# New latencies in the planner of an attention and MLP kernel, and its static rules chosen anew

## The chip, the cores and the metric

The kernel runs on one core of a Trainium2 chip. The time is that of the device for one execution, in microseconds (us), the median of several runs. Lower is better.

## The reference

The input is a sequence x of 2048 rows of 640 values in bf16. What is computed is x + s * g.

```
xn = layernorm(x)
q, k, v = split(xn @ wqkv)                 # 32 heads of 20 values
s  = softmax(q k^T / sqrt(20)) v @ wo      # attention, per head 2048 x 2048 scores
u  = gelu(layernorm(xn)^T @ w1 + b1)       # MLP over the rows (2048 -> 1536 -> 2048)
g  = silu((u @ w2 + b2)^T)
out = x + s * g
```

## The kernel before

**The work.** The 32 heads form 8 groups of 4 heads; a *pass* is one group and 512 query rows, and there are 33 passes, the last two of half a pass each. A pass goes through 16 chunks of 128 keys. One head, one chunk and 512 queries make a *unit*: a score product of 128 x 512 that fills one PSUM bank. There are 2,048 units. The four heads of a group lie in the four row strips of TensorE (PE), so that up to four units with different heads run side by side.

**Two ways through a unit.** Most units (1,552) go to ScalarE (ACT): one activation takes the exponential of two or three banks (`emit_exp`, L1308) into `pt_sb`, a ring of 20 tiles. The other 496 go to VectorE (DVE): `emit_op1` (L1319) makes 16-bit integers out of one bank that are read as bf16 values of an approximate exponential, and `emit_top` (L1357) makes three shifted copies of four such units (a quad); four products with scaled values (`vs_sb`) take their weighted sum. PE then multiplies `pt_sb` and `dt_sb` by the values (`pv_mm`, L1376), with four column tiles side by side, into one accumulator bank. After a pass DVE transposes and normalizes it (`ep_steps`, L1492 to L1518).

**The banks.** Of 8 PSUM banks six form two groups of three, (0, 1, 2) and (3, 4, 5). A *visit* (`do_st`, `emit_st`, L1279) is a run of score products into one group: three units for ACT, or two for ACT and one whose bank is lent to DVE, at times with one more in bank 7. While ACT works on one group, PE may fill the other. Bank 6 is the accumulator; bank 7 serves the other products.

**The other work on PE.** Between visits PE does the value products, the projections of Q, K and V (L633, L746 before the exponentials are in full flow; L648, L691 later), both MLP layers (L648), and the output projection (L965, L970). The later projections and the MLP use column tiles too. Where PE has nothing to do, `emit_fill` (L1393) adds four products with zero weights, so that its activity does not fall; `emit_warm` (L1403) does the same ahead of the first products. `row_piece` (L656) cuts one step of a projection into four row strips and hangs one of them beside a visit.

**The order of the work.** A planner in the kernel's own Python code decides it. It keeps a clock for each engine (`Prog.T`), adds a cost for every instruction, and notes for each one when others may use what it wrote (`fin`, plus `lat` by engines). In a loop it takes the engine whose next possible instruction comes first, and that engine's candidate with the best priority. The order of each engine's instructions is fixed by this; on the chip semaphores alone hold them back. For PE, `act_deadline` gives the time by which the next visit has to begin for ACT not to run dry, and `pe_cands` offers other work only where it ends, by the planner's costs, before that.

Three terms of these costs matter here. `lat` (L66) is added between an end on one engine and a start on another. `pe_cost` (L460) adds a price where the tiling of PE changes: row strips for a visit ("st"), column tiles ("pv"), whole array ("full"). `emit_st` (L1262) spreads the time of a visit over its products, and `_add` sets the `fin` of a PE instruction to its end and 170 ns. Before the change, the first products of a visit cost 20 ns each and the last one the rest of 216 ns:

```
cost = (first if i == 0 else 0.0) + (20.0 if i < n - 1 else tot - 20.0 * (n - 1))
```

The class constants are the static rules: `D_GUARD` (units that have to be left for ACT in a pass before a new DVE quad may be started in it, and the mark for giving up bank 7 at the end), `MLP_A`, `MLP_B` (passes over which the MLP is spread), `ROOM` (free tiles in the ring below which value products come first), `FGAP` (ns of slack from which a fill is allowed), `ACTP` (priority of the MLP's activation steps), `PARTS` (pieces in which a quad's four value products may be issued), `V1A`, `V1B` (passes over which the later V projection is spread).

Of the kernel before, what the change touches and what calls it, by code (L numbers as in the profile page):

```python
# [39 lines left out]
class Prog:  # L40
# [23 lines left out]
        self.alog = []  # L64

    def lat(self, eng, src):  # L66
        return (40.0 if eng == "dve" else 0.0) if src == eng else self.LAT[eng] + (79.0 if eng == "act" and src == "pe" else 57.0 if eng == "dve" and src == "pe" else 0.0)

    def ready(self, eng, reads=(), writes=()):
        r = 0.0  # L70
# [195 lines left out]
class _Kern:  # L266
# [13 lines left out]
    AK = (1.0, 0.83984375, 0.70703125, 0.59375)  # L280
    MEAN4 = 4.159829600672171
    LOG2E = 1.4426950408889634
    D_GUARD = 8
    MLP_A, MLP_B = 2.6, 23.0
    QK_LEAD = 6.0
    SLACK, MINJ = 0.0, 640.0
    ROOM = 3
    ROWM, ROWP, ROWN = 5, 2, 400
    lastrow = None
    MERGE = False  # L290
# [10 lines left out]
    LONE, DLEAD, DRIDE = False, 0.0, 400.0  # L301
    NQS = 3
    CONFL = True
    FILL, FGAP, FACT = True, 40.0, 0.6
    LATE = 1.0
    LEND, LEND_MIN = 1800.0, 3
    SHARE = True
    VPRIO = 25.0
    QAT = (0.0, 0.0, 0.0, 0.0)
    ACTP = 22.0  # L310
    COLS = True
    NTILE, NLIVE, EARLY = 8, 3, True
    QC = ((0.5, 3.0), (3.2, 6.4), (9.0, 13.5), (14.0, 18.0), (19.0, 22.0))
# [6 lines left out]
        ("MINJ", (640.0, 320.0, 1000.0)),  # L320
        ("ROOM", (3, 6, 0)),
        ("DRIDE", (400.0, 150.0, 700.0)),
        ("LEND", (1800.0, 1300.0, 2400.0, 700.0, 0.0)),
        ("PARTS", ((2,), (2, 1), (3, 1), (1,), ())),
        ("LATE", (2.0, -9.0, 99.0)),
# [6 lines left out]
        ("GROT", (1, 0)),  # L332
    )
    PLAN = ()
    PARTS = (2,)
    DX = (1, 2, 3)
    V1A, V1B = 1.2, 3.0

    def __init__(self, nc, A_x, A_wqkv, A_wo, B_w1, B_b1, B_w2, B_b2, out):
        self.nc = nc  # L340
# [70 lines left out]
    def schedule(self):  # L411
        pr, t, nc = self.prog, self.t, self.nc
# [28 lines left out]
        def ps(b, n=512, off=0):  # L441
            return ps_all[:, b * 512 + off:b * 512 + off + n]
# [17 lines left out]
        def pe_cost(mode, c):  # L460
            if pe_mode[0] != mode:
                pe_mode[0] = mode
                return c + max(0.0, (105.0 if mode == "st" else 113.0) - max(0.0, pr.T["pe"] - pr.pe_end))
            return c

        def dma(fn, reads, writes, name, nbytes, over=()):
# [399 lines left out]
        UP = NB * GH  # L866
# [3 lines left out]
        units, dunits = [], []  # L870
# [149 lines left out]
        bankq = []  # L1020
# [38 lines left out]
        nclaim = [0]  # L1059
# [71 lines left out]
        dop1 = []  # L1131
# [68 lines left out]
        def d_claimable():  # L1200
            if not self.DON:
                return None
            if tfree and dlive[0] < self.NLIVE:
# [3 lines left out]
                for q in (q0, q0 + 1):  # L1207
                    if q >= NP:
                        continue
                    G, p = passes[q]  # L1210
                    if q == q0 and a_left(q) < self.D_GUARD:
                        continue
# [49 lines left out]
        def emit_st(lst, banks):  # L1262
            n = len(lst)
            first = pe_cost("st", 0.0)
            gs = {}
            for (q, c, g) in lst:
                gs[g] = gs.get(g, 0) + 1
            tot = 216.0 * max(gs.values())
            for i, (q, c, g) in enumerate(lst):
                G, p = passes[q]  # L1270
                slot = G % 2
                bk = banks[i]
                cost = (first if i == 0 else 0.0) + (20.0 if i < n - 1 else tot - 20.0 * (n - 1))
                np_ = len(units[q][c])
                for ch, col, m, off, _ in units[q][c]:
                    lhsT = qk_sb[32 * g:32 * g + 32, slot, 1, ch * 128:(ch + 1) * 128]
                    rhs = qk_sb[32 * g:32 * g + 32, slot, 0, col:col + m]
                    outp = ps(bk, m, off)
                    pr.pe(lambda e, outp=outp, lhsT=lhsT, rhs=rhs, g=g: e.matmul(outp, lhsT, rhs, start=True, stop=True,  # L1279
                                                                                tile_position=(32 * g, 0)),  # L1280
                          reads=qslots(slot, p, col, m, g) + [S_(kslot(slot, ch, g))] + ([S_(f"qkp_{g}")] if slot else []),
                          writes=[bank_slot[bk]], name=f"st{q}_{c}_{g}", cost=cost / np_, w=53.0 / np_)
                nclaim[0] += 1
                if st_left[G] == NTB * UP:
                    done.add(f"STbegin{G}")
                st_left[G] -= 1
                if st_left[G] == 0:
                    done.add(f"ST{G}")
# [259 lines left out]
        for w in (1, 0):  # L1548
            src = A_wqkv[:, 640 * w + 256:640 * w + 640].rearrange("(kc p) f -> p kc f", p=P)
# [64 lines left out]
        for j in range(FC):  # L1614
# [4 lines left out]
            if j % 2:  # L1619
                add_job(f"a1_{j}", act_steps(1, j), tuple(f"m1_{i}_{q}" for i in (j - 1, j) for q in (0, 1)), self.ACTP)  # L1620
            if j % 2 == 1 and j // 2 + 2 < FC // 2:
# [5 lines left out]
        for j in range(NB):  # L1627
# [4 lines left out]
            if j % 2:  # L1632
                add_job(f"a2_{j}", act_steps(2, j), tuple(f"m2_{i}_{q}" for i in (j - 1, j) for q in (0, 1)), self.ACTP)
            if j % 2 == 1 and j // 2 + 2 < NB // 2:
                k = j // 2 + 2
                add_job(f"w2_{k}", [dma_w2(k), ("tag", f"w2_{k}")], (f"m2_{j}_0", f"m2_{j}_1"), 40.0)
        tot = sum(x[3] for x in ml)
# [10 lines left out]
        for gb in range(4):  # L1648
            src = A_x[0, gb * 512:(gb + 1) * 512, :].rearrange("(b p) d -> p b d", p=P)
# [122 lines left out]
        def pe_cands(T):  # L1772
# [110 lines left out]
            room = sum(not b for b in pt_busy) - pend  # L1883
            if room < self.ROOM:
                o = [x for x in pv if x[1] <= T + 1.0 and x[4] > 0]
# [204 lines left out]
            return a - done_cost["act"], pe - done_cost["pe"], d - done_cost["dve"]  # L2090

        self.loads = loads
        guard = 0
        win = 0
        while True:
# [10 lines left out]
            if nomore:  # L2106
                for b in act_banks:
                    if b not in bank_off and b not in lent and not any(b in x[1] for x in pexp):
                        bank_off.add(b)
                        if len(tbank) < NL:  # L2110
                            done.add(f"tbank{len(tbank)}")
                            tbank.append(b)
            if (nomore or (a_cur[0] == NP - 1 and a_left(NP - 1) < self.D_GUARD)) and d_cur[0] is None and not dop1:
                if not bankq and JB not in busybanks and JB not in bank_off:
# [18 lines left out]
            r, e = bt  # L2133
# [46 lines left out]
```

## Time and profile before

| what | us |
|---|---|
| median of 3 runs | 756.44 (756.05 to 757.03) |
| the profiled execution | 757.3 |
| its span, first to last instruction | 755.5 |
| ACT busy | 730.5, of it exponentials 711.7 (683) |
| DVE busy | 720.5 |
| PE busy | 709.7 |
| GpSimd (POOL) busy | 15.5 |

The span is the time from the first to the last instruction of the profiled execution; 1.8 us lie around it. A busy time is the union of an engine's instruction records. PE's matmuls are pipelined and their ends are modelled, so that its busy time is not a measure of how full it is. Records of successive activations overlap (the mean record of a 128x1024 exponential is 1106 ns long), so that an idle time of less than that overlap does not show in busy time, and starts have to be compared. The granted TensorE clock is 1.000 in the mean of the span.

### The profile page before, as it was taken

To read this page: it belongs to the slowest core of one execution; us is meant where nothing else is said; L and a number is where in the kernel's file an instruction comes from. 1 tells how busy PE (TensorE), PEld (TensorE's weight loads), DVE (VectorE), ACT (ScalarE), POOL (GpSimd) and SP (SyncE) were. 2 spreads that over 40 slices of the span, in tenths; PEclk is the share of its full clock that TensorE was granted. 3 is DMA by queue.
4 is the path that set the end of the run, shared out by engine and by line. 5 is a ranking of instruction groups with operands and counts; after the bars stand their busy time and mean duration, and the time that the engine had idled before them with its cause. 6 is when DMAs were issued, how large, how long until landed. Compare 5 with 4: busy or idle time off the path is not lost.

```text
span 755.5 us, 23583 instructions
## 1 busy us (share of the span) xinstructions
PE 709.7 (94%) x10508; PEld 242.5 (32%) x10520; DVE 720.5 (95%) x1321; ACT 730.5 (97%) x708; POOL 15.5 (2%) x23
## 2 busy tenths in 40 slices
PE   8889999999999999999999998999999999999997
PEld 7332222232233323332232232323233332332333
DVE  8899989999998999999999999999999999999997
ACT  5899999999999999999999999999999999999994
POOL 4200000000000000000000000000000000000000
PEclk9999999999999999999999999999999999999999
DMA  9745211110121301312011104122225510041012
GB/s 234 146 113 63 63 22 37 20 37 5 40 60 20 76 6 45 85 34 46 13 31 27 30 7 119 19 51 50 60 80 88 130 39 30 2 152 47 26 35 71
DMA packets 119738, 42.66 MB, mean 56 GB/s; under 512 B 79172, under 2 KB 118468, under 8 KB 119588
## 3 DMA queue, kind: packets, MB, share of 16 engines
q1 hardware_dynamic: 119636, 41.15, 23.6%
q8 instruction: 82, 1.34, 0.8%
q14 instruction: 20, 0.16, 0.1%
HBM read 26.37 MB, written 10.22 MB: 48 GB/s over the span
## 4 chain that ended last, share of the span: by engine, by line
ACT 84%; PE 11%; DVE 3%; DMA 1%; SPq 0%; issue 0%
ACT pt_sb L1308 82%; PE ps_all L648 4%; PE ps_all L1279 4%; PE ps_all L1376 3%; ACT zt_sb L849 1%; ACT zt_sb L844 1%; DMA regA<-in_A_x_dram 1%; DVE regC L568 1%; DMA xnT_sb<-regC 0%; PE ps_all L965 0%; PE ps_all L633 0%; DVE bst_sb L530 0%; DVE bst_sb L532 0%; DVE dt_sb L1319 0%; DVE v_sb L1114 0%
## 5 line engine op out<-in xcount | busy, mean ns | idle before, releaser
L1308 ACT ACTIVATE pt_sb<-ps_all 128x1024 bf16<-128x1024 f32 (+2 forms) x683 | 711.7, 1220 | 6.1 <-PE ps_all L1279 3.8
L1319 DVE TENSOR_SCALAR dt_sb<-ps_all 128x512 uint16<-128x512 f32 x496 | 327.7, 679 | 18.8 <-PE ps_all L1279 9.7
L1279 PE MATMUL ps_all<-qk_sb 32*128 32x512 bf16 (+1 forms) x2128 | 268.6, 376 | 32.5 <-ACT pt_sb L1308 28.9
L1357 DVE TENSOR_SCALAR dt_sb<-dt_sb 128x2048 uint16<-128x2048 uint16 x372 | 239.2, 683 | 1.6
L1279 PEld LDWEIGHTS ps_all<-qk_sb 32*128 32x128 bf16 x2128 | 68.3, 91 | 289.5 <-ACT pt_sb L1308 243.8
L1376 PE MATMUL ps_all<-pt_sb,v_sb 128*21 128x512 bf16 (+1 forms) x1616 | 127.0, 374 | 2.3 <-DVE v_sb L1114 1.0
L1376 PE MATMUL ps_all<-dt_sb,vs_sb 128*21 128x512 bf16 (+1 forms) x1536 | 124.1, 375 | 0.1
L648 PE MATMUL ps_all<-regB,regA 128*32 128x128 bf16 (+1 forms) x1492 | 63.6, 299 | 0.0
L648 PE MATMUL ps_all<-regC,regA 128*32 128x128 bf16 (+1 forms) x1448 | 62.5, 296 | 0.1
L1376 PE MATMUL ps_all<-dt_sb,v_sb 128*21 128x512 bf16 (+1 forms) x512 | 49.0, 378 | 0.3 <-issue 0.3
L1376 PEld LDWEIGHTS ps_all<-pt_sb,v_sb 128*21 128x21 bf16 x1616 | 32.9, 91 | 50.9 <-issue 32.5
L648 PE MATMUL ps_all<-xnT_sb,wqk_sb 128*32 128x512 bf16 x640 | 45.6, 382 | 0.2 <-DVE qs_sb L1117 0.2
L1376 PEld LDWEIGHTS ps_all<-dt_sb,vs_sb 128*21 128x21 bf16 x1536 | 30.0, 91 | 33.1 <-issue 22.9
L648 PEld LDWEIGHTS ps_all<-regB,regA 128*32 128x32 bf16 x1492 | 26.9, 96 | 25.2 <-issue 12.9
L648 PEld LDWEIGHTS ps_all<-regC,regA 128*32 128x32 bf16 x1448 | 26.2, 96 | 24.9 <-issue 14.0
L656 PE MATMUL ps_all<-regC,regA 32*128 32x512 bf16 x88 | 33.9, 385 | 0.0
L965 PE MATMUL ps_all<-wv_sb,xnT_sb 128*128 128x128 bf16 (+1 forms) x150 | 25.4, 296 | 1.9 <-issue 1.1
L1500 DVE STREAM_TRANSPOSE tr_sb<-ps_all 128x512 f32<-128x512 f32 x31 | 21.9, 706 | 0.0
L648 PE MATMUL ps_all<-wv_sb,xnT_sb 128*32 128x480 bf16 x320 | 21.1, 369 | 0.0
L1376 PEld LDWEIGHTS ps_all<-dt_sb,v_sb 128*21 128x21 bf16 x512 | 12.5, 90 | 24.3 <-issue 21.0
L648 PEld LDWEIGHTS ps_all<-xnT_sb,wqk_sb 128*32 128x32 bf16 x640 | 13.2, 95 | 18.4 <-issue 8.1
L823 DVE TENSOR_SCALAR zt_sb<-ps_all,b2h_sb 128x512 bf16<-128x512 f32 (+1 forms) x32 | 17.2, 540 | 0.6 <-PE ps_all L648 0.6
(88 smaller groups left out, 347.5 us busy)
## 6 DMA issues: line engine op xcount, KB each, us to landing
regA<-in_B_w_dram SPq DMA_DIRECT2D x6, 1024.0 KB
regA<-in_B_w_dram SPq DMA_DIRECT2D x8, 768.0 KB
qk_sb<-qk_scratch_dram SPq DMA_DIRECT2D x56, 80.0 KB
qk_scratch_dram<-qs_sb SPq DMA_DIRECT2D x32, 128.0 KB
regA<-in_A_x_dram SPq DMA_DIRECT2D x6, 640.0 KB
ok_scratch_dram<-on_sb SPq DMA_DIRECT2D x96, 20.0 KB
out_dram<-regC SPq DMA_DIRECT2D x3, 640.0 KB
wqk_sb<-in_A_wqkv_dram SPq DMA_DIRECT2D x2, 480.0 KB
```

What stands on the lines that cost most here:

```text
L568: steps.append(("dve", lambda e, b=b: e.tensor_scalar(regC[:, b, :], regC[:, b, :], st_sb[:, 6, b:b + 1], None, ALU.mult), [S_("r2"), S_(f ...
L648: fns.append(lambda e, c=c, e_=e_: e.matmul(oc(c, e_), lhsT[:, c:e_], rhs, start=start, stop=stop, tile_position=(0, c)))
L656: row = lambda g: (lambda e: e.matmul(oc(0, 128), lhsT[32 * g:32 * g + 32, :], rhs[32 * g:32 * g + 32, :], start=False, stop=False, tile_p ...
L823: steps.append(("dve", lambda e, z=z, i=i, jj=jj: e.tensor_scalar(z[:, c0:c0 + n], ps(bk, n, i * n), 0.5, bias[:, jj:jj + 1], ALU.mult, AL ...
L844: steps.append(("act", lambda e: e.activation(tt_, tt_, AF.Tanh, scale=1.5957691216), [stt], [stt], f"th{j}", ac(n)))
L965: steps.append(("pe", lambda e, c=c: e.matmul(ap, oT_sb[:, c, b * 128:(b + 1) * 128], wo_ap[:, c, c0:c0 + n], start=(opens and c == 0), st ...
L1279: pr.pe(lambda e, outp=outp, lhsT=lhsT, rhs=rhs, g=g: e.matmul(outp, lhsT, rhs, start=True, stop=True, tile_position=(32 * g, 0)), reads=q ...
L1308: tk = pr.act(lambda e: e.activation(outp, inp, AF.Exp, scale=math.log(2.0) / 128.0), reads=[bank_slot[b] for b in banks[:n]], writes=[S_( ...
L1319: tk = pr.dve(lambda e: e.tensor_scalar(w, src, WOFF, 0.0, ALU.add, ALU.max), reads=[bank_slot[bk]], writes=[S_(f"dt{d['tl'][0]}_{g}")], n ...
L1357: tk = pr.dve(lambda e: e.tensor_scalar(dst, src, dk, None, ALU.add), reads=[S_(f"dt{b}_{g}") for b in inb for g in range(4)], writes=[S_( ...
L1376: pr.pe(lambda e: e.matmul(outp, lhsT, rhs, start=(k == 0), stop=last, tile_position=(0, 32 * g)), reads=reads, writes=[bank_slot[AB]], na ...
L1500: steps.append(("dve", lambda e: e.transpose(tr_sb[:, :], ps(AB)), [bank_slot[AB]], [S_("tr")], f"epT{q}", 632.0))
```

## The change

It has four parts.

1. `lat`: from a PE result to ACT 95 ns instead of 134, to DVE 100 instead of 112.
2. `pe_cost`: a tiling change costs 105 ns less half of the time that PE has waited just before; it was 105 or 113 less all of that time.
3. `emit_st`: the products of a visit start 4 ns apart, and each one is taken as done 332 ns after its own start (358 where its bank is DVE's), with 216 ns more for each earlier product of the same head in the visit and with the price of the tiling change for the first one.
4. The static rules get other values. A lambda, `self.backlog`, is added that nothing in the kernel calls; the lists `OPTS` and `PLAN` have no effect, as `PLAN` is empty.

```diff
-        return (40.0 if eng == "dve" else 0.0) if src == eng else self.LAT[eng] + (79.0 if eng == "act" and src == "pe" else 57.0 if eng == "dve" and src == "pe" else 0.0)
+        return (40.0 if eng == "dve" else 0.0) if src == eng else self.LAT[eng] + (40.0 if eng == "act" and src == "pe" else 45.0 if eng == "dve" and src == "pe" else 0.0)
...
-    D_GUARD = 8
-    MLP_A, MLP_B = 2.6, 23.0
+    D_GUARD = 16
+    MLP_A, MLP_B = 2.6, 24.0
...
-    ROOM = 3
+    ROOM = 6
...
-    FILL, FGAP, FACT = True, 40.0, 0.6
+    FILL, FGAP, FACT = True, 0.0, 0.6
...
-    ACTP = 22.0
+    ACTP = 30.0
...
-    PARTS = (2,)
+    PARTS = (3, 1)
...
-    V1A, V1B = 1.2, 3.0
+    V1A, V1B = 0.5, 4.0
...
-                return c + max(0.0, (105.0 if mode == "st" else 113.0) - max(0.0, pr.T["pe"] - pr.pe_end))
+                return c + max(0.0, 105.0 - 0.5 * max(0.0, pr.T["pe"] - pr.pe_end))
...
             tot = 216.0 * max(gs.values())
+            own = {x[2] for x in dop1}
+            gs = {}
             for i, (q, c, g) in enumerate(lst):
+                late = (358.0 if banks[i] in own else 332.0) + 216.0 * gs.get(g, 0)
+                gs[g] = gs.get(g, 0) + 1
...
-                cost = (first if i == 0 else 0.0) + (20.0 if i < n - 1 else tot - 20.0 * (n - 1))
+                cost = (first if i == 0 else 0.0) + (4.0 if i < n - 1 else tot - 4.0 * (n - 1))
...
-                for ch, col, m, off, _ in units[q][c]:
+                for n_, (ch, col, m, off, _) in enumerate(units[q][c]):
...
-                    pr.pe(lambda e, outp=outp, lhsT=lhsT, rhs=rhs, g=g: e.matmul(outp, lhsT, rhs, start=True, stop=True,
+                    t = pr.pe(lambda e, outp=outp, lhsT=lhsT, rhs=rhs, g=g: e.matmul(outp, lhsT, rhs, start=True, stop=True,
...
+                    t.fin = t.t0 + late + (first if i + n_ == 0 else 0.0)
```

No line of the change issues an instruction by itself. The order of the instructions on PE, DVE, ACT and the DMA queue is another one throughout.

More of the change, by code (lines that the diff above doesn't have):

```diff
@@ L1278, in emit_st @@
                     outp = ps(bk, m, off)
-                    pr.pe(lambda e, outp=outp, lhsT=lhsT, rhs=rhs, g=g: e.matmul(outp, lhsT, rhs, start=True, stop=True,
-                                                                                tile_position=(32 * g, 0)),
+                    t = pr.pe(lambda e, outp=outp, lhsT=lhsT, rhs=rhs, g=g: e.matmul(outp, lhsT, rhs, start=True, stop=True,
+                                                                                    tile_position=(32 * g, 0)),
                           reads=qslots(slot, p, col, m, g) + [S_(kslot(slot, ch, g))] + ([S_(f"qkp_{g}")] if slot else []),
                           writes=[bank_slot[bk]], name=f"st{q}_{c}_{g}", cost=cost / np_, w=53.0 / np_)
+                    t.fin = t.t0 + late + (first if i + n_ == 0 else 0.0)
                 nclaim[0] += 1
@@ L2092, in schedule @@
         self.loads = loads
+        self.backlog = lambda: sum(1 for j in bankq if j.at <= nclaim[0] / UP)
         guard = 0
```

## The prediction

> **What bounds the kernel now.** The first view is the page: the busy line, then the chain that ended last.
>
> ```profile
> PE 709.7 (94%) x10508; PEld 242.5 (32%) x10520; DVE 720.5 (95%) x1321; ACT 730.5 (97%) x708; POOL 15.5 (2%) x23
> ACT 84%; PE 11%; DVE 3%; DMA 1%; SPq 0%; issue 0%
> ```
>
> Three engines are over 94% busy, but the chain runs along ACT for 84% of the span, nearly all of it the exponentials (L1308). Busy time hides short stalls, since an exponential's record overlaps the next one's, so the second view is the starts of successive activations in the trace. Undisturbed, a 128x1024 exponential (two score units, a "double") is followed after 903 ns and a 128x1536 one (a "triple") after 1330 ns, though their records last 1106 and 1524 ns. ACT's work is thus 495 x 0.903 + 187 x 1.330 + one single of 0.48 + 14 tanh of 1.16 = 712.4 us. The first exponential starts at 11.9 us and the last is over at 744.8: 732.9 us. With 1.1 us of copies inside, 19 us are stalls: 4.5 us before 50 us, some 14 us spread evenly after it (0.7 to 2.2 us in every 50), the rest is rounding. So there are three places to win or lose: the start, the 14 us, and the 10.7 us after the last exponential.
>
> The third view shows what such a stall is, the timeline around 61 us.
>
> ```profile
> 60.68 0.39 PE L1279 MATMUL ps_all<-qk_sb 32*128 32x512 bf16 x3
> 61.00 0.40 PE L1376 MATMUL ps_all<-dt_sb,v_sb 128*21 128x512 bf16 x4
> 61.22 0.39 PE L1376 MATMUL ps_all<-dt_sb,vs_sb 128*21 128x512 bf16 x4
> 61.44 0.60 PE L1376 MATMUL ps_all<-pt_sb,v_sb 128*21 128x512 bf16 x8
> 61.98 0.39 PE L1279 MATMUL ps_all<-qk_sb 32*128 32x512 bf16 x3
> 62.45 1.33 DVE L1319 TENSOR_SCALAR dt_sb<-ps_all 128x512 uint16<-128x512 f32 x2
> ```
>
> L1279 is a visit: three score products side by side. Four matmuls with column tiles (L1376) take 0.22 us together (61.00, 61.22, 61.44): a **slot**. From the visit to the slots after it 0.32 us pass, 0.10 more than a slot, and as much on the way back: the tiling change. The visit at 61.98 comes after four slots; ACT's next exponential starts at 62.41 in the trace, 0.43 us after it, and DVE's first step at 62.45, 0.47 after it. ACT had been free since 62.20: it stalled 0.21 us. The chain around 136 us shows the same with five slots of a projection:
>
> ```profile
> 133.18 2.27 ACT pt_sb L1308 x2
> 135.45 0.05 issue
> 135.50 0.39 PE ps_all L1279 x3
> 135.89 1.12 PE ps_all L648 x20
> 137.02 0.37 PE ps_all L1279 x3
> 137.39 3.27 ACT pt_sb L1308 x3
> ```
>
> **What the Trainium skill says.** "TensorEngine Tiling (Array Packing)", Key Properties: changing the tiling mode drains TensorE; the trace agrees, 0.10 us each way. "TensorE: Matmul & The Clock Gate", Part 3 (The mechanism): tiles on different rows start about 4 ns apart and matmuls end in program order; the trace agrees on the starts (a visit's products lie 430, 427 and 424 ns ahead of a double), and ACT's 0.43 us holds whether it reads two or three of them, so they do end together. "ScalarE: Activation LUTs", What ACT_TABLE_LOAD costs: 186 ns + 0.833 per column less 93 of overlap, an estimate of 946 ns for a double; the trace has 903 and decides.
>
> **The rule for a stall.** A bank group is free when its exponential's record ends, 1106 - 903 = 203 ns after the next one starts; the visit follows 54 ns later at the earliest, and what reads it starts 430 ns after. Between two visits PE may therefore spend the two exponentials before less 687 ns. For two doubles: 1806 - 687 - 216 (visit) - 2 x 97 (changes) = 709 ns, three slots (649). Four slots (865) are some 156 ns too many. With a triple among the two, five fit.
>
> **The change part by part.**
>
> *The planner's reckoning* (lat, pe_cost, emit_st). It issues nothing; it alters when the planner thinks banks are full. Before, the products of a visit end one after the other: for a double whose third product goes to DVE the plan has ACT ready at 20 + 20 + 170 + 134 = 344 ns, for a triple at 520. The trace has 430 and 440. The new formula gives 332 + 4 + 95 = 431 and 435; for DVE 358 + 8 + 100 = 466 against 464 to 466. So doubles, 495 of the 683 exponentials, were taken for 86 ns quicker than they are, and the plan put four slots where they do not fit. That the change of tiling hides half of a wait I can't read from a view.
>
> *The order that results*, counted in the two built orders. Work is the same: 2,128 score and 3,664 value matmuls, 496 DVE units, 14 tanh. What differs:
> - Exponentials: 491 doubles and 190 triples, no single: 443.4 + 252.7 = 696.1 against 696.2 us. One 128x512 copy (L1116) goes from DVE to ACT: +0.5. Net **+0.4**.
> - Between 30 exponentials after the start and 12 before the end, four or more slots stand between two doubles 38 times before and 21 after. I priced every interval by its kind (the two exponentials, the slots) with the mean stall that its kind has in the trace of before: four slots between doubles 32 times, 4.9 us, 153 ns each, now 17 times, 2.6 us; five or more 6 times, 0.9, now 4, 0.6; four after triple and double 19 times, 1.1, now 10, 0.6; all others 7.1, now 6.4. Sum 14.0 to 10.2: **-3.8**.
> - The remaining four-slot pieces are placed by a clock that fits: of the 32, eight cost 21 ns or less. Bounds 0 and -2.6 (none of them stalls); I take **-0.8**.
> - Tiling changes 1,257 to 1,292: 35 x 0.1 = 3.5 us more of PE. Fills (L1393) 200 to 244 matmuls, 11 slots, 2.4 us; row pieces (L656) 132 to 120, three whole steps back in the open, 0.6 us. In that middle part PE's work goes from 610 to 616 us, its reserve against ACT from 55 to 46. Cover: that reserve. If stalls grow as the reserve shrinks, 14 x (55/46 - 1) = 2.7; bounds 0 and +2.7, I take **+1.0**.
> - DVE: same steps less one; it has 712 busy of 743 us and is fed by the same visits. Nothing, as long as the visits come no later.
> - SP: the same 306 DMAs. Granted clock is full throughout before (PEclk all 9), and fills grow: nothing.
>
> *The start.* At 30.23 ACT waited 1.35 us:
>
> ```profile
> 28.02 0.49 DVE L1114 CAST v_sb<-ps_all 128x320 bf16<-128x320 f32 x1 [0.20 <-PE ps_all L746]
> 28.57 0.72 PE L633 MATMUL ps_all<-xnT_sb,wp_sb 128*128 128x256 bf16 x5 [0.59 <-DVE v_sb L1114]
> 30.23 1.45 ACT L1308 ACTIVATE pt_sb<-ps_all 128x1536 bf16<-128x1536 f32 x1 [1.35 <-PE ps_all L1279]
> ```
>
> The key projection (L633) stood behind ten value matmuls and their copy. In the new order it comes ahead of them, and the visit too. One DVE quad leaves pass 0, so ACT does four more units early and four fewer later. Bounds -1.5 and +1.0 (another input may be late next: the transposed rows, or the copy now on ACT); I take **-0.8**.
>
> *The end.*
>
> ```profile
> 745.53 0.63 PE L1376 MATMUL ps_all<-dt_sb,vs_sb 128*21 128x256 bf16 x16
> 746.45 0.45 DVE L1492 STREAM_TRANSPOSE tr_sb<-ps_all 128x256 f32<-128x256 f32 x1 [1.38 <-PE ps_all L1376]
> 751.40 0.41 DVE L1730 TENSOR_TENSOR regC<-ps_all,regC 128x256 bf16<-128x256 f32 x1
> ```
>
> The last value products wait for DVE's tiles, 1.65 us lie between the last exponential and the transpose. In the new order DVE's last unit is five exponentials before the end instead of two, and after the last visit stand 32 value matmuls instead of 56 and 15 instead of 19 of 512 columns: 0.7 + 0.9 us less of PE. Bounds -1.5 and +0.5; I take **-1.0**.
>
> **Sum**: 0.4 - 3.8 - 0.8 + 1.0 - 0.8 - 1.0 = -5.0 us. Against the profiled execution, 757.3 (span 755.5 and 1.8 around it), that is 752.3; it stands 0.9 above the median of the three runs, 756.44, so I forecast **751.4**.
>
> **Rivals.**
> 1. *PE becomes the bound* (slower). The 35 tiling changes and 11 fills stand on the path of the visits; between two doubles two slots leave only 277 ns, and back-to-back visits without a change, with which PE caught up, fall from 64 to 45. Then the shorter pieces spare nothing. With half of the added 6.5 us on ACT: +3.3 + 0.4 - 1.8 = +1.9, 758.3; all of it, 761.5. It decides from 1.4 us of it landing there on. Against it: in the trace two-slot intervals between doubles stall by 4 ns in the mean. Chance 0.16.
> 2. *The stalls only move*: 10.2 us become 14 again by visits late for DVE's sake (DVE has 31 us idle in all). Middle 0, start and end -1.8, copy and density +1.4: 756.0. Chance 0.08.
> 3. *More is won*: all bounds at their good end, +0.4 - 3.8 - 2.6 - 1.5 - 1.5 = -9.0: 747.4. Chance 0.14.
> That the reckoning is not what it says would show as rival 1: but its latencies are those of the trace.
>
> **The numbers.** Forecast 0.62, and rival 3 with it, are faster by over 0.2% (1.5 us, about what a measurement here tells from no change): 0.76. Rival 2 is 0.08, rival 1 is 0.16. The range reaches from rival 3 to rival 1's first value: 747.5 to 758.3.
>
> **What will show it.** Right: sums of the starts with 10 us or less of stall after 50 us; few stalls of four slots between doubles; no idle time of over 1 us on ACT near 30 us; under 10 us after the last exponential. Wrong: ACT waiting for visits after two-slot pieces; a granted clock under 1.00; DVE idle for L1279 well over 9.7 us.

## The result and the profile after

| | median, us | range | ratio to before |
|---|---|---|---|
| before, in the same session | 756.76 | 756.05 to 757.37 | |
| after | 754.03 | 753.77 to 755.22 | 0.9967 [0.9955, 0.9979] |

The change makes the kernel 2.7 us faster; 5.0 were forecast. The profiled execution of after took 754.1 us (span 752.3), 3.2 less than that of before. Its page, the busy line and the chain that ended last:

```profile
PE 716.3 (95%) x10561; PEld 243.6 (32%) x10561; DVE 719.0 (96%) x1320; ACT 730.0 (97%) x707; POOL 15.3 (2%) x23
ACT 76%; PE 18%; DVE 6%; issue 0%; DVEq 0%
```

ACT is as busy as before; PE has 6.6 us more, and the chain leaves ACT more often for it. As in the prediction, busy time can't say where 3 us went. So all that follows rests on one ledger per run, taken from the starts of ACT's activations in the trace. A stall is the time from one start to the next, less what the first takes undisturbed (903.5 ns for a double, 1330.5 for a triple, 1160 for a tanh, 264 to 493 for a copy); the floor is the sum of the undisturbed times from the first exponential to the last; the end is what follows the last one.

| us | before | after | difference | forecast |
|---|---|---|---|---|
| first exponential starts | 11.93 | 12.09 | +0.16 | start -0.8 |
| stalls before 50 us | 5.13 | 5.58 | +0.45 | (same) |
| stalls 50 to 650 us | 12.61 | 10.54 | -2.07 | middle -3.6 |
| stalls after 650 us | 1.30 | 1.16 | -0.14 | (same) |
| floor | 713.60 | 713.98 | +0.38 | +0.4 |
| end | 10.91 | 8.97 | -1.94 | -1.0 |
| sum: span | 755.48 | 752.32 | -3.16 | -5.0 |

**The start.** The timeline of ACT in after; the bracket at the end of a line is the idle time before it and what released it:

```profile
28.33 8.18 ACT L1313 ACTIVATE pt_sb<-ps_all 128x1536 bf16<-128x1536 f32 x6 [0.20 <-PE ps_all L1283]
37.46 0.60 ACT L1116 ACTIVATE qk_sb<-ps_all 128x512 bf16<-128x512 f32 x1 [0.95 <-PE ps_all L633]
39.99 10.72 ACT L1313 ACTIVATE pt_sb<-ps_all 128x1536 bf16<-128x1536 f32 x10 [1.93 <-PE ps_all L1381]
```

The wait of 1.35 us near 30 us is gone, as forecast. In its place two others stand 7 and 10 us later. The second is of a kind that the prediction did not count: the exponential waits for value products (L1381), not for scores. All 20 tiles of the ring `pt_sb` are full until those products have read one.

**The middle.** One such ring wait was in before too, the largest stall of its middle: 1.59 us from start to start, 1.42 as idle time in this line of its timeline:

```profile
593.75 2.85 ACT L1308 ACTIVATE pt_sb<-ps_all 128x1024 bf16<-128x1024 f32 x3 [1.42 <-PE ps_all L1376]
```

After has none between 50 and 650 us. Split into ring waits and the rest (waits for visits), before has 1.9 + 10.7 us there and after 0 + 10.5. (Two small ring waits, of 77 and 252 ns, are among before's 1.9.) So nearly all that the middle gained is the loss of its ring waits, and the visits, at which the new reckoning is aimed, gained 0.16 us.

**The end.** The last part of after's chain of waits:

```profile
743.86 0.60 PE ps_all L1381 x16
744.46 0.02 issue
744.48 0.46 DVE tr_sb L1497
...
747.59 0.34 DVE regC L1735
```

The transpose follows the last value products at once, at 744.48 instead of 746.45, and the addition that stood at 751.40 (L1730, now L1735) at 747.51 (747.59 in the chain). That is 3.9 us earlier, 1.2 of it because the last exponential is over earlier. The addition behind it (L1737) then takes 1.01 us where it took 0.29, and of the lead 3.2 us are left at DVE's last step.

### The profile page after: what moved, and what is told of

The parts are those of the page before. It is cut to its first block, busy times and chain, and to the rows that moved or that the text cites. A ratio compares the mean times of both kernels' runs of the same rounds, so it can differ in the third digit from the quotient of the medians.

```text
span 752.3 us, 23672 instructions
## 1 busy us (share of the span) xinstructions
PE 716.3 (95%) x10561; PEld 243.6 (32%) x10561; DVE 719.0 (96%) x1320; ACT 730.0 (97%) x707; POOL 15.3 (2%) x23
## 4 chain that ended last, share of the span: by engine, by line
ACT 76%; PE 18%; DVE 6%; issue 0%; DVEq 0%
ACT pt_sb L1313 74%; PE ps_all L1381 5%; PE ps_all L1283 5%; PE ps_all L648 5%; DVE dt_sb L1324 1%; PE ps_all L1408 1%; ACT zt_sb L849 1%; DVE dt_sb L1362 1%; ACT zt_sb L844 1%; DVE bst_sb L532 1%; DVE bst_sb L530 1%; DVE regC L548 1%; PE ps_all L965 1%; PE ps_all L633 0%; DVE v_sb L1114 0%; PE ps_all L746 0%
## 5 line engine op out<-in xcount | busy, mean ns | idle before, releaser
L1313 ACT ACTIVATE pt_sb<-ps_all 128x1024 bf16<-128x1024 f32 (+1 forms) x681 | 711.2, 1242 | 4.9 <-PE ps_all L1283 2.1
L1283 PE MATMUL ps_all<-qk_sb 32*128 32x512 bf16 (+1 forms) x2128 | 269.1, 376 | 26.4 <-ACT pt_sb L1313 22.9
L1283 PEld LDWEIGHTS ps_all<-qk_sb 32*128 32x128 bf16 x2128 | 68.4, 91 | 280.9 <-ACT pt_sb L1313 226.4
L1381 PE MATMUL ps_all<-dt_sb,vs_sb 128*21 128x512 bf16 (+1 forms) x1536 | 130.7, 376 | 0.9 <-DVE dt_sb L1362 0.5
L1381 PE MATMUL ps_all<-pt_sb,v_sb 128*21 128x512 bf16 (+1 forms) x1616 | 127.0, 374 | 1.9 <-DVE v_sb L1114 0.9
L648 PE MATMUL ps_all<-regC,regA 128*32 128x128 bf16 (+1 forms) x1472 | 65.5, 297 | 0.0
L1381 PEld LDWEIGHTS ps_all<-dt_sb,vs_sb 128*21 128x21 bf16 x1536 | 33.4, 90 | 51.7 <-issue 31.2
L1381 PE MATMUL ps_all<-dt_sb,v_sb 128*21 128x512 bf16 (+1 forms) x512 | 49.2, 377 | 0.1
L1381 PEld LDWEIGHTS ps_all<-pt_sb,v_sb 128*21 128x21 bf16 x1616 | 30.9, 90 | 49.2 <-issue 35.9
L648 PEld LDWEIGHTS ps_all<-regB,regA 128*32 128x32 bf16 x1480 | 27.4, 96 | 23.3 <-issue 10.9
L965 PE MATMUL ps_all<-wv_sb,xnT_sb 128*128 128x512 bf16 (+1 forms) x160 | 27.3, 301 | 0.0
L656 PE MATMUL ps_all<-regC,regA 32*128 32x512 bf16 x64 | 24.6, 384 | 0.0
L656 PE MATMUL ps_all<-regB,regA 32*128 32x512 bf16 x56 | 21.5, 384 | 0.0
L1381 PEld LDWEIGHTS ps_all<-dt_sb,v_sb 128*21 128x21 bf16 x512 | 13.0, 90 | 20.6 <-issue 14.2
L1398 PE MATMUL ps_all<-wp_sb,zw_sb 128*21 128x512 bf16 (+1 forms) x244 | 19.4, 373 | 0.0
```

The lines of the kernel that those rows point to most:

```text
L648: fns.append(lambda e, c=c, e_=e_: e.matmul(oc(c, e_), lhsT[:, c:e_], rhs, start=start, stop=stop, tile_position=(0, c)))
L656: row = lambda g: (lambda e: e.matmul(oc(0, 128), lhsT[32 * g:32 * g + 32, :], rhs[32 * g:32 * g + 32, :], start=False, stop=False, tile_p ...
L965: steps.append(("pe", lambda e, c=c: e.matmul(ap, oT_sb[:, c, b * 128:(b + 1) * 128], wo_ap[:, c, c0:c0 + n], start=(opens and c == 0), st ...
L1283: t = pr.pe(lambda e, outp=outp, lhsT=lhsT, rhs=rhs, g=g: e.matmul(outp, lhsT, rhs, start=True, stop=True, tile_position=(32 * g, 0)), rea ...
L1313: tk = pr.act(lambda e: e.activation(outp, inp, AF.Exp, scale=math.log(2.0) / 128.0), reads=[bank_slot[b] for b in banks[:n]], writes=[S_( ...
L1381: pr.pe(lambda e: e.matmul(outp, lhsT, rhs, start=(k == 0), stop=last, tile_position=(0, 32 * g)), reads=reads, writes=[bank_slot[AB]], na ...
```

## The experiments

A *piece* is what PE does between two visits; a *full* piece has four slots between two doubles, one more than the prediction's rule allows. Letters for theories in the expectations are each run's own. Times are medians; before had 756.6 to 756.7 us beside these runs, and 757.9 beside the last two. After's 754.03 was measured beside a before of 756.76 and not again.

### At the start and in the middle, with after's order fixed

For e1 to e4 and f3, f4 and g4 after's plan was made as it is, noted, edited and laid down again with its waits worked out anew, so that nothing moves but what is named:

```diff
             self.schedule()
+            self.prog = pr = _again(nc, _edit(pr.log))
             pr.final_waits()
```

**e1, a slot moved.** In 16 of the 17 four-slot pieces between doubles the last slot goes behind the visit that follows.

```diff
+        last = r["gap"][-4:]
...
+        for m in last:
+            log.remove(m)
...
+        log[end + 1:end + 1] = last
```

> The changed kernel in its own fixed order, but in 16 of its 17 four-slot pieces between two doubles the last slot stands behind the visit that follows. Theory A (what the new order lost again is at these pieces, because it reaches them without a lead; they cost 229 ns each in its trace): most of 16 x 0.23 = 3.7 us goes, less new stalls of some tens of ns where the next piece grows to three slots; 751.3 us, between 750.5 and 752. Theory B (PE as a whole is the bound, the stall only moves to the next visit): 754.0, within 0.7.

Measured: 753.85 us, ratio 0.9967 [0.9954, 0.9980]; stalls 50 to 650 us 10.56 (after 10.54). Nothing is won, as theory B had it. PE's timeline shows it at one place, first after, then e1 (L1405 is its visit, L1503 its value products, L770 its projections):

```profile
377.37 0.61 PE L1381 MATMUL ps_all<-dt_sb,vs_sb 128*21 128x512 bf16 x8
377.81 0.61 PE L1381 MATMUL ps_all<-pt_sb,v_sb 128*21 128x512 bf16 x8
378.35 0.39 PE L1283 MATMUL ps_all<-qk_sb 32*128 32x512 bf16 x3
378.67 1.05 PE L648 MATMUL ps_all<-xnT_sb,wqk_sb 128*32 128x512 bf16 x16
379.65 0.39 PE L1283 MATMUL ps_all<-qk_sb 32*128 32x512 bf16 x3
```

```profile
377.45 0.39 PE L1503 MATMUL ps_all<-pt_sb,v_sb 128*21 128x512 bf16 x4
377.78 0.39 PE L1405 MATMUL ps_all<-qk_sb 32*128 32x512 bf16 x3
378.10 0.40 PE L1503 MATMUL ps_all<-pt_sb,v_sb 128*21 128x512 bf16 x4
378.32 1.04 PE L770 MATMUL ps_all<-xnT_sb,wqk_sb 128*32 128x512 bf16 x16
379.29 0.39 PE L1405 MATMUL ps_all<-qk_sb 32*128 32x512 bf16 x3
```

Here another full piece stands behind the full one: four slots and then four became three and then five. The stalls there went from 270 and 18 ns to 56 and 176. It is much the same at the others, though in 11 of the 17 the next piece has only one to three slots: at the 17 pieces the stalls fell from 3.9 to 1.1 us, and at the next two exponentials they rose by 2.1 and 0.7. So a full piece is not a misplaced slot. Over the two or three visits from it on PE has no time left, and the slot delays one of them wherever it stands.

**e2, the start.** V of keys 1024 to 1279, its copy and its products go ahead of the Q projection of rows 512 to 1023 and its copy on ACT.

```diff
+    put(v, copied)
+    put(ve, hs[2])
+    put(pv, visit)
+    put(q, pv[-1])
+    put(qe, pick("act", "exp(0, 13, 0)")[0])
```

> The changed kernel in its own fixed order, but at 35 to 40 us the value projection of keys 1024 to 1279, its copy and its products go ahead of the query projection of rows 512 to 1023 and its copy, which share one PSUM bank. Theory A (the start lost what the early visit had won, since the ring of exponentials was full behind this bank): the wait of 1.9 us before the exponential at 39.99 us falls under 0.3, and the time by 1.5 to 2.0 us to 752.3. Theory B (another input comes late next at the start): 754.0, within 0.5.

Measured: 753.38 us (752.91 to 753.45), ratio 0.9951 [0.9939, 0.9963], the fastest kernel here that computes everything, 0.65 below after. Stalls before 50 us 5.11 (after 5.58), less than expected. ACT's timeline of e2:

```profile
37.52 1.45 ACT L1405 ACTIVATE pt_sb<-ps_all 128x1536 bf16<-128x1536 f32 x1 [1.11 <-PE ps_all L1473]
...
42.01 1.94 ACT L1405 ACTIVATE pt_sb<-ps_all 128x1024 bf16<-128x1024 f32 x2 [1.14 <-PE ps_all L1375]
```

The ring wait shrinks from 1.93 to 1.11 us, and another wait of 1.14 comes at 42.0. Bank 7 passes from V to Q to the next V, with a copy between each two: in e2's trace the next V projection waits 0.36 us for ACT's copy of Q (at 39.58), its products 0.26 us for the copy of V (at 41.04), and the late visit stands behind them.

**g4, more of it.** The next two V projections and their products go ahead of Q too.

```diff
-    put(q, pv[-1])
-    put(qe, pick("act", "exp(0, 13, 0)")[0])
+    put(q, pv2[-1])
+    put(qe, pick("act", "exp(0, 13, 3)")[0])
```

> After in its fixed order, with V of keys 1024 to 1535 (four V projections instead of the two of e2), their copies and products ahead of the Q projection of rows 512 to 1023 and its copy. If bank 7, through which these pass one after the other, and the full ring of 20 tiles of probabilities set the waits of 35 to 42 us, the second wait of e2 (1.14 us at 42.0) goes too: stalls before 50 us 4.0 (after 5.6, e2 5.1), 752.4 us. If the Q copy or its first readers are then late, stalls stay at 5.1, 753.4.

Measured: 754.61 us, ratio 0.9972 [0.9961, 0.9984]: 1.2 slower than e2. Now ACT's copy of Q waits 1.66 us, at 44.67. (This profiled execution is 2.5 us above the median, with an early wait of 2.07 at 22.02 that no edit touched; only the waits after 35 us are read.) Three orders of the same five steps gave 2.9, 2.3 and 2.8 us of waits (0.95 + 1.93; 1.11 + 1.14; 1.11 + 1.66): the wait moves along the chain through bank 7.

**e3 and e4, the fills.** The 42 fill slots (168 matmuls) between the 30th exponential and the 12th from the end are left out (e3), or issued twice (e4).

```diff
+        if x["name"] == "pvz" and 30 <= seen < n - 12:
+            continue
```

> The changed kernel in its own fixed order without the 42 fill slots (168 of 244 zero matmuls) between the 30th exponential and the 12th before the end. Theory A (fills stand in time that PE would have waited): 754.0, from 0 to 0.8 us less, as long as the granted clock stays at 1.00. Theory B (PE's density is the price that I set too low): 9.1 us of PE work go, and 2 to 3 us of time.

> The changed kernel in its own fixed order, each of these 42 fill slots issued twice: 9.1 us more of PE work, all of it in intervals between visits. Theory A: fills stand where there was time for more than one slot, so a third of them or fewer delay a visit: 1 to 3 us more. Theory B: nearly all of it lands on ACT, 6 to 9 us more.

Measured: e3 757.26 us (754.25 to 758.80 in 14 runs), 0.9999 [0.9987, 1.0011]; its granted clock has a mean of 0.990 to 0.999, and the run with 0.999 took 754.25, as long as after. e4 758.46, 1.0021 [1.0013, 1.0029], with a clock of 0.999. So, as far as that one run tells, a fill costs nothing where the planner puts it, and without the fills the clock is not held; a second one beside it adds: of 42 x 0.216 = 9.1 us of work, 4.4 land on the time, between the two theories. Rival 1's half was a fair price for work put where there is no room.

**f3 and f4, one slot less.** Four value products are left out in 14 of the four-slot pieces (f3), or in 14 pieces of one or two slots nearby (f4).

```diff
+    full = [a for a in range(1, len(runs) - 1) if slots(runs[a]) == 4]
...
+    return [x for x in log if id(x) not in gone]
```

> After in its fixed order, with one slot (four products of probabilities and V) left out in 14 of the 17 four-slot pieces between doubles; these 56 of the products are missing from the output. Theory A, room at the piece (a slot too many there costs ACT about 0.2 us, one elsewhere nothing): stalls fall by 14 x (0.229 - 0.032) = 2.8 us. Theory B, PE is short of time over the whole stretch, so half of any PE work shows (as 9.1 us of fills cost 4.4): 14 x 0.216 x 0.5 = 1.5 us.

> After in its fixed order, with one slot of products left out in each of 14 pieces of one or two slots between doubles, the nearest to those of the run f3 that have no four-slot neighbour; these 56 products are missing from the output. Theory A, room at the piece: nothing, within 0.3 us. Theory B, PE short of time over the whole stretch: -1.5 us, as in f3.

Measured: f3 752.43 us, ratio 0.9942 [0.9928, 0.9955]; stalls 50 to 650 us 8.92, that is -1.62. f4 753.99, 0.9961 [0.9947, 0.9975]; stalls 10.50, nothing. The same work was taken away. Where a piece has room it is worth nothing; where it is full it is worth 1.62 / 14 = 116 ns of a slot's 216. Theory B of that pair falls; of theory A the place is right and the size not. At the 17 full pieces themselves the stalls fell from 3.9 to 1.5 us, but some 0.8 us came back at other exponentials, 0.2 each at 518.4 and 524.3 us.

### The two halves of the change

**f1, the reckoning alone.** Parts 1 to 3 of the change, all rules as before.

```diff
-    D_GUARD = 16
+    D_GUARD = 8
...
-    FILL, FGAP, FACT = True, 0.0, 0.6
+    FILL, FGAP, FACT = True, 40.0, 0.6
...
-    PARTS = (3, 1)
+    PARTS = (2,)
```

> The kernel after with its four edits of the scheduler's reckoning (waits of ACT and DVE behind PE, tiling change, ends of a visit's products) and all static rules (ROOM, PARTS, FGAP, D_GUARD, ACTP, MLP_B, V1A, V1B) as before. The order has 26 four-slot pieces between doubles (before 32, after 17). Theory A, the reckoning carries the gain, as the prediction had it: -2.5 to -3.5 us against before, stalls of 50 to 350 and 350 to 650 us near after's 3.8 and 6.7. Theory C, the count of full pieces in the order decides, whoever makes it: 6 fewer of them at 0.15 us are -0.9 us in the middle, with start and end as they fall: -0.5 to -1.5 us in all.

**f2, the rules alone.** The old `lat`, `pe_cost` and `emit_st` with the new rules. Against after, a piece of the line of `lat`:

```diff
...
-self.LAT[eng] + (40.0 if eng == "act" and src == "pe" else 45.0 if
+self.LAT[eng] + (79.0 if eng == "act" and src == "pe" else 57.0 if
...
```

> The kernel before with its old reckoning and all static rules as after. The order has 16 four-slot pieces between doubles (before 32, after 17). Theory A, the reckoning carries the gain: within 0.5 us of before, as the rules then work on a wrong clock. Theory C, the count of full pieces decides: as fast as after or faster in the middle (stalls between 50 and 650 us 10.0 to 10.5 us against 12.6 before), -2 to -3 us in all.

Measured: f1 760.65 us, 1.0051 [1.0038, 1.0063]; f2 760.44, 1.0045 [1.0031, 1.0059]. Alone they are 4.1 and 3.8 us slower than before; together they are 2.7 faster. Both theories fall. The ledgers say different things of the two. In f1 the floor is 717.29 instead of 713.60 us, because its plan gives DVE eight units fewer. The page's rows of exponentials and of DVE's first step, after and f1:

```profile
L1313 ACT ACTIVATE pt_sb<-ps_all 128x1024 bf16<-128x1024 f32 (+1 forms) x681 | 711.2, 1242 | 4.9 <-PE ps_all L1283 2.1
L1324 DVE TENSOR_SCALAR dt_sb<-ps_all 128x512 uint16<-128x512 f32 x496 | 328.4, 683 | 15.9 <-PE ps_all L1283 8.9
```

```profile
L1313 ACT ACTIVATE pt_sb<-ps_all 128x1024 bf16<-128x1024 f32 (+1 forms) x679 | 714.8, 1237 | 5.7 <-PE ps_all L1283 3.1
L1324 DVE TENSOR_SCALAR dt_sb<-ps_all 128x512 uint16<-128x512 f32 x488 | 322.8, 681 | 24.6 <-PE ps_all L1283 15.8
```

Eight units on ACT for eight on DVE: 3.3 us of floor against after, while DVE's idle time ahead of this step is 8.7 us longer, most of it for want of visits (15.8 instead of 8.9). In f2 the floor is right, but stalls 50 to 650 us are 13.94 and the end 12.94. Its 16 four-slot pieces are as few as after's 17, so that their count did not make it. In its profiled execution 1.4 us are three stalls between 456 and 460 us, where the granted clock stood at half for 3.4 us from 455.5; its two runs with a clock of 1.000 took 759.94 and 760.22 us, so that this is not what makes it slow. In seven places, 2.60 us, PE comes late to a visit because it had waited for DVE's transpose of the accumulator (`tr_sb`) before the first products of the next pass. The waits of the whole run, f2 and then after:

```profile
PEld ps_all L1376 <- DVE tr_sb L1500: 6.0, 14, 1.0
PE ps_all L1376 <- DVE tr_sb L1500: 2.1, 7, 0.7
```

```profile
PEld ps_all L1381 <- DVE tr_sb L1505: 2.7, 9, 0.5
```

**g1, the reckoning and FGAP = 0. g2, after with D_GUARD = 8. g3, before with D_GUARD = 16.** Each is one rule, and each makes a new plan.

```diff
-    FILL, FGAP, FACT = True, 40.0, 0.6
+    FILL, FGAP, FACT = True, 0.0, 0.6
```

> The four edits of the reckoning and, of the rules, FGAP = 0 alone; the order gives DVE 496 halves of a visit again (488 in f1, 496 in before and after) and has 17 four-slot pieces. Theory D, f1 was slow because 8 halves more stood on ACT: the floor is 714.0 instead of 717.3 us and the time falls by 3.3 us from f1, to 757.3; the tail after the last exponential stays at 11. Theory E, the plans are a lottery of equal chances: stalls of 50 to 650 us anywhere between 10 and 14 us, which alone moves the time between 755.5 and 759.5.

```diff
-    D_GUARD = 16
+    D_GUARD = 8
```

> After with D_GUARD = 8 (all else as after; the plan is made anew, with 12 four-slot pieces and 70 fills). Theory F, D_GUARD makes the short end: what lies after the last exponential goes from 9.0 back to 10.9 us, 755.9 in all if nothing else moves. Theory E, the lottery of plans: the end falls anywhere between 9 and 13 us, and the stalls of the middle move by as much.

```diff
-    D_GUARD = 8
+    D_GUARD = 16
```

> Before with D_GUARD = 16 alone, the old reckoning (35 four-slot pieces, 32 in before). Theory F, D_GUARD makes the short end: 10.9 falls to 9.0 us, 754.8 in all if nothing else moves. Theory E: the end anywhere between 9 and 13 us.

Measured: g1 760.36 us (1.0048 [1.0035, 1.0060]), g2 767.79 (1.0154 [1.0140, 1.0169]), g3 768.96 (1.0163 [1.0143, 1.0184]). In g1 the floor is back at 713.98, as theory D had it, but the time did not follow: end 12.19, and two ring waits of 2.9 us. D_GUARD does not by itself make the short end: with 16 in the old reckoning it is 22.4 us, with 8 in the new one 13.8, both outside of what theory E had allowed too. (The last 13.6 of the 22.4 us ran at half the clock; g3's runs spread from 767.13 to 771.25.) In g2 the time goes into the ring; this is a line of its waits from 50 to 740 us (us in total, times, longest):

```profile
ACT pt_sb L1313 <- PE ps_all L1381: 6.8, 3, 3.2
```

### Null edits

**h1 to h4.** The two waits that `lat` adds behind PE are made 1 ns longer or shorter, in before and in after. In h3 and h4, and in i2 below, the 40 ns that `lat` gives DVE behind itself move by 1 ns with them. The piece of the line that differs, for h1:

```diff
...
-(79.0 if eng == "act" and src == "pe" else 57.0 if eng == "dve"
+(80.0 if eng == "act" and src == "pe" else 58.0 if eng == "dve"
...
```

> Before with its two reckoned waits behind PE 1 ns longer (80 and 58 for 79 and 57), which says nothing new of the chip but makes another plan (35 four-slot pieces, 496 halves on DVE). Theory E, plans are a lottery: 2 to 12 us slower than before, as every edit of f1, f2 and g1 to g3 was, because before was the pick of many. Theory A, the reckoning's truth carries the gain: within 1 us of before, 756 to 758.

> Before with its two reckoned waits 1 ns shorter (23 four-slot pieces, 500 halves on DVE: a floor 1.6 us lower). Theory E: 2 to 12 us slower than before. Theory A: within 1 us of 756.7, or 1.6 below it by the floor.

> After with its two reckoned waits 1 ns longer (41 and 46 for 40 and 45; 16 four-slot pieces, 492 halves on DVE: a floor 1.6 us higher). Theory E: 2 to 12 us slower than after. Theory A: 754 to 756.5, still below before.

> After with its two reckoned waits 1 ns shorter (12 four-slot pieces, 492 halves on DVE: a floor 1.6 us higher). Theory E: 2 to 12 us slower than after. Theory A: 754 to 756, below before. Of both theories the stalls from 50 to 650 us tell what the reckoning is worth in itself: the mean of h3, h4 and after against the mean of h1, h2 and before.

**i1 and i2.** The same, in f2 (1 ns longer) and in f1 (1 ns shorter); for i2:

```diff
...
-(40.0 if eng == "act" and src == "pe" else 45.0 if eng == "dve"
+(39.0 if eng == "act" and src == "pe" else 44.0 if eng == "dve"
...
```

> The kernel of f2 (old reckoning, new rules) with its two reckoned waits 1 ns longer (14 four-slot pieces, 492 halves on DVE). Stalls from 50 to 650 us so far: old reckoning and old rules 12.6, 14.4, 12.0; new and new 10.5, 10.2, 8.8; one of the two alone 12.1 (f1) and 13.9 (f2). Theory G, it takes both: 12 to 15 us here. Theory H, f2 was an unlucky plan and the rules carry the gain, with their few four-slot pieces: 9 to 11 us.

> The kernel of f1 (new reckoning, old rules) with its two reckoned waits 1 ns shorter (28 four-slot pieces, 488 halves on DVE). Theory G, it takes both: stalls from 50 to 650 us 11.5 to 14. Theory A, the reckoning carries the gain and f1 was an unlucky plan: 9 to 11 us.

Measured, with the plans from above, by what each contains. "Visits" are stalls from 50 to 650 us without ring waits; "output" is the number of output projection matmuls (L965) that start after the last exponential has.

| plan | reckoning | FGAP | other rules | visits | ring | floor | end | output | time | ratio |
|---|---|---|---|---|---|---|---|---|---|---|
| before | old | 40 | old | 10.7 | 1.9 | 713.6 | 10.9 | 33 | 756.7 | |
| h1 | old + 1 ns | 40 | old | 12.5 | 1.9 | 713.6 | 11.8 | 35 | 759.8 | 1.0039 [1.0031, 1.0047] |
| h2 | old - 1 ns | 40 | old | 11.7 | 0.3 | 711.8 | 38.4 | 110 | 782.4 | 1.0322 [1.0282, 1.0363] |
| g3 | old | 40 | old, D_GUARD 16 | 13.1 | 0.1 | 713.6 | 22.4 | 71 | 769.0 | 1.0163 [1.0143, 1.0184] |
| f2 | old | 0 | new | 13.9 | 0 | 713.5 | 12.9 | 49 | 760.4 | 1.0045 [1.0031, 1.0059] |
| i1 | old + 1 ns | 0 | new | 13.3 | 0 | 715.2 | 17.5 | 68 | 768.1 | 1.0131 [1.0100, 1.0162] |
| f1 | new | 40 | old | 12.1 | 0 | 717.3 | 11.1 | 33 | 760.7 | 1.0051 [1.0038, 1.0063] |
| i2 | new - 1 ns | 40 | old | 12.4 | 0 | 717.3 | 13.5 | 38 | 764.5 | 1.0083 [1.0054, 1.0112] |
| g1 | new | 0 | old | 10.1 | 2.9 | 714.0 | 12.2 | 39 | 760.4 | 1.0048 [1.0035, 1.0060] |
| g2 | new | 0 | new, D_GUARD 8 | 10.4 | 8.0 | 714.0 | 13.8 | 50 | 767.8 | 1.0154 [1.0140, 1.0169] |
| after | new | 0 | new | 10.5 | 0 | 714.0 | 9.0 | 31 | 754.0 | 0.9967 [0.9955, 0.9979] |
| h3 | new + 1 ns | 0 | new | 10.2 | 0 | 715.7 | 10.1 | 34 | 756.6 | 0.9996 [0.9989, 1.0003] |
| h4 | new - 1 ns | 0 | new | 8.8 | 0 | 715.8 | 17.2 | 63 | 765.4 | 1.0110 [1.0087, 1.0133] |

Three things follow.

First, a nanosecond in the planner costs 2.6 to 26 us against its parent, in all six null edits. (For i2, by its ratio 2.4 us slower than f1, the intervals overlap.) After with 1 ns more (h3) is as fast as before. Theory E of h1 to h4 holds, and for h2 its 12 us were too few. What changes most is the end. Of h2, a piece of the chain of waits:

```profile
754.80 1.27 PE ps_all L965 x5
756.09 0.70 DVE regC L980
756.84 1.27 PE ps_all L965 x5
758.13 0.70 DVE regC L980
```

The output projection goes through one bank: PE makes 512 columns in 1.27 us, DVE takes them away in 0.70, and PE waits for that. The more of it is left for the end, the longer the end: 31 to 35 matmuls go with 9.0 to 11.8 us, 38 to 50 with 12.2 to 13.8, 63 to 71 with 17 to 22, 110 with 38.

Second, under that scatter the middle does shift. The five plans with the new reckoning and FGAP = 0 have 8.8 to 10.5 us of stalls at visits, mean 10.0. The eight others have 10.7 to 13.9, mean 12.5; before is the lowest of them. They are fewer than they look, as plans 1 ns apart have long stretches in common: before and h1 have 352 pieces in a row with the same number of matmuls, of some 620, f2 and i1 400 and after and h4 360 of some 640. By families it is three (means 9.8, 10.1, 10.4) against five (11.6, 11.7, 12.3, 13.1, 13.6). Neither half does it, as theory G of i1 and i2 had it: new with 40 has 12.1 and 12.4, old with 0 has 13.9 and 13.3, of which 1.4 and 1.5 us stand at a drop of the clock to half (at 455.5 and 456.0 us); 12.5 and 11.9 would still be above the five. That of the new rules it is FGAP which matters rests on g1 alone, and how a threshold for fills acts on visits was not traced.

Third, ring waits and the split of units between DVE and ACT differ from plan to plan without such an order: 0 to 8.0 us, and a floor of 711.8 to 717.3.

## Why the prediction was wrong

The direction was right, and 1.8 of the 5.0 us were not there (3.16 in the ledger). That the gain is as large as it is, is in part luck: the ring waits (-1.9) and the end (-1.9) are more than all of it. No term of the prediction stood for the first, the second went beyond its bound, and 1 ns less in before (h2) takes its ring waits from 1.9 to 0.3 us and its end from 10.9 to 38.4. Nor does the reckoning carry it, as the prediction's first part had it: alone (f1) it is 4.1 us slower.

- **The exponentials and the copy, +0.4**: measured +0.38.
- **The repricing of intervals, -3.8, and the clock that fits, -0.8, less the density, +1.0: -3.6 in all.** Measured -2.2. This is the main step that failed. The four-slot pieces did fall from 32 to 17, but I priced the rest at the old mean of 153 ns, and took 0.8 off: 1.8 us. They stall 229 ns each, 3.9 us, 2.1 more. My reason for taking 0.8 off was that eight of the old ones cost 21 ns or less; such harmless ones are what the new plan no longer has. e1 and f3 show why a price for each kind doesn't hold: a stall belongs to a stretch of pieces. The four-slot pieces after a triple and a double came out at 0.2 instead of 0.6, five or more at 0.65 as priced (0.6). All other intervals came to 7.0 instead of 6.4.
- **Hidden in "all others"** was the ring wait of 1.59 us at 593.8: it stands at an interval of one slot. I had spread it over a class with its mean. It was one event with one cause, and its end is most of what the middle gained. Without it the others of before were 5.5 us, so that they rose by 1.5: three slots between doubles from 1.7 to 2.6 us, two from 0.5 to 1.0. What the full pieces gave came back there. Why the new plan has no ring wait after 50 us isn't settled: g2 has four, with ROOM and PARTS as in after.
- **The density, +1.0**: f4 says that work in short pieces costs nothing, f3 and e4 that about half of it shows where a piece has no room. No run weighs the term by itself.
- **The start, -0.8**: measured +0.6, inside the bound of +1.0. "Another input may be late next" is what happened, the V products behind bank 7 and the copy on ACT. The sign I took was wrong: I followed one wait to its end and not the chain through bank 7 behind it. f1 has both waits too (0.96 and 1.93 us), and f2 does not wait for the ring there, so that the ring wait at least comes with the reckoning. Before 50 us the stalls of before were 5.1 in the ledger where I had read 4.5. Of the +0.6, +0.16 is the first exponential, which started at 11.4 to 12.1 us in eight runs in which nothing of after's order was touched before 35 us.
- **The end, -1.0**: measured -1.9, 0.4 beyond its bound of -1.5. The steps named for it (fewer value products behind the last exponential, no wait for DVE's tiles ahead of the transpose) are in the trace. Nulls and single rules show that it is also the term that the plan's accidents move most: after's end is the shortest of 13.
- **Rival 1** did not come: two-slot intervals between doubles stall 5 ns in the mean, the clock is 0.999. Its sign, ACT waiting for L1283 after short pieces, is absent. **Rival 2**, stalls that only move, is what the start shows, and the visits of the middle against the plan before; the end and the ring wait made the gain.
- Of the signs given ahead, "10 us or less of stall after 50 us" failed (11.7), "under 10 us after the last exponential" held, and "no idle time of over 1 us near 30 us" held by its letter while 1.93 us stood at 40.

The working rested on the order that the change gives, counted out. Reasoned from the edits alone ("truer latencies, so fewer overfull pieces"), f1 would have been forecast as a gain.

## What to carry to other kernels

Where a program decides the order, judge a change to its costs by the order that comes out, and run one or two null edits (1 ns) of both kernels before any credit is given to the idea: here they moved the time by up to ten times the effect, and only one row of the ledger, the stalls at visits, differs in the mean by more (2.5 us) than these edits scatter it (up to 1.8). Price single large stalls one by one with their cause, and use class means only for the many small ones. Where PE works without reserve over several visits, moving a slot to the next piece did nothing; taking work out helped there only, in all by half of its length.

## What the hardware showed that was not expected

Without fills the granted clock fell although PE never stood still for long. The table of stretches of e3 (per engine the busy time and the instructions; then the granted clock, DMA share and GB/s):

```profile
440.00:450.00 10.00, 9.70 (x206) 3.95 (x205) 10.00 (x20) 10.00 (x10) 0.00 (x0) 1.00 0.60 159
450.00:455.00 5.00, 2.88 (x29) 0.69 (x25) 5.00 (x11) 5.00 (x6) 0.00 (x0) 0.99 0.17 15
455.00:460.00 5.00, 4.89 (x37) 0.98 (x37) 4.13 (x8) 4.35 (x5) 0.00 (x0) 0.50 0.16 28
460.00:465.00 5.00, 5.00 (x63) 1.22 (x63) 4.01 (x7) 3.95 (x5) 0.00 (x0) 0.83 0.00 0
```

Five microseconds with PE busy for 58% by its records (2.88 of 5.00), its matmuls at most 1.16 us from start to start, were followed by half the clock, for 6.8 us from 454.9. The Trainium skill ("TensorE: Matmul & The Clock Gate", Part 1) has the clock fall to half after an idle window of about 3.4 us; the half is as measured, but no idle stretch of that length lies ahead of this dip. A second dip began at 519.7 and lasted 3.41 us. The two begin 64.85 us apart, 19 times 3.41, and in the 3.41 us ahead of each PE was busy for 60% (2.05 and 2.06 us). From 357.0 on it was busy for only 1.73 of 3.41 us, and the clock stayed full; but these lie across two stretches of that grid, with 72% and 71%. So in this trace the dips follow the share of busy time in the stretches of a fixed grid. A threshold does not come out of it: g2 has a stretch of 59% on the grid of its own dip, at 607.0, without one.

Between 450 and 550 us, with both dips, ACT's stalls came to 5.6 us in e3 and 2.0 in after.
